# Loading half of y from ScalarE's queue, x's first rows last, and releasing the stores by a product

## The chip, the core and the metric

The kernel runs on one core of a Trainium2 chip. The metric is the device time of one execution in microseconds (us); three runs of the kernel before gave 119.63, 119.76 and 119.88, a median of 119.76. A core has compute engines with an instruction stream each: TensorE (PE in the profile), VectorE (DVE), ScalarE (ACT), GpSimd (POOL) and SyncE (SP). Data moves between the chip's main memory (HBM) and the on-chip memory (SBUF, 128 partitions) through 16 DMA engines. SP and ACT each own a DMA queue; an instruction on SP or ACT puts one transfer into its queue, where all 16 DMA engines work on it. Engines wait for each other and for transfers through semaphores.

## The reference

`x` and `y` are bf16 arrays of 1024 x 16 x 512, `gamma` is a bf16 row of 512. The result is

```python
def reference(x, y, gamma):
    return x + gamma * y
```

So 16.78 MB of `x` and 16.78 MB of `y` are read and 16.78 MB are written. Per element there is one product and one sum.

## The kernel before

The 16384 rows of 512 elements are spread over the 128 partitions, 128 rows for each partition (1 KB a row). "Row" below means such a row of a partition, 0 to 127, so a row stands for 128 KB over all partitions. `BLOCKS` (line 7) cuts HBM in three, so that a partition's rows 0 to 4, 4 to 68 and 68 to 128 each lie together in HBM. A transfer takes part or all of one block, and in one partition it is a single run of bytes: 4 KB for rows 0 to 4, 64 KB for rows 4 to 68.

All of `y` has its place in SBUF (`y_sb`, 128 rows) and is overwritten first by the product and then by the sum; stores go out of it. `x` has only 76 rows of space (`x_sb`); the last number of an `x` load in the lists is the row of `x_sb` at which it lands, so later loads of `x` reuse the place of earlier ones and have to wait for the sums that read those.

Four lists are the whole schedule.

- `SP` (line 12) is the order in which SP issues transfers: y 0-4, y 4-68, x 4-68, y 68-128, x 68-120, x 120-128. `ring` (line 113) writes them out. For an `x` load it waits for the sums that free its place (line 126): x 68-120 for the sum of rows 24 to 68, and x 120-128 for the sum of rows 0 to 8.
- `ACT` (line 20) is ACT's order: x 0-4, gamma, and then the stores of rows 4-68, 0-4 and 68-128.
- `PIECES` (line 9) cuts the rows for VectorE into 0-8, 8-24, 24-68, 68-120 and 120-128, and `DVE` (line 28) is the order of its products ('m', line 180) and sums ('a', line 189): products 0, 1, 2; sums 2, 0, 1; products 3, 4; sums 3, 4.
- `EARLY` (line 22) says how many issues of SP and of ACT are put at the very start of the program, ahead of the engines' common start. `HOLD` and `AHEAD` (line 24) hold SP's third and ACT's second issue, and the first product, until y 0-4 has landed: TensorE waits for that landing (line 147) and then tells SP, ACT and VectorE (line 149).

`gamma` lands as a single row on one partition. TensorE multiplies it by a column of ones (line 152), so that it stands in all 128 partitions of PSUM, and VectorE copies it to `gamma_sb` (line 154). No product can start before that copy.

The stores are kept back by `RELEASE` (line 26). TensorE waits until x 68-120 has landed (line 157) and then raises `s_go`, for which ACT waits ahead of its first store (line 123), and `s_rel`, for which VectorE waits ahead of the sum of rows 68-120 (line 167). Beside that each store waits for the sums of its rows.

Of the kernel before, what the change touches and what calls it, by code (L numbers as in the profile page):

```python
# [5 lines left out]

BLOCKS = [4, 64, 60]

PIECES = [8, 16, 44, 52, 8]


SP = [
    ('y', 0, 4),
    ('y', 4, 68),
    ('x', 4, 68, 4),
    ('y', 68, 128),
    ('x', 68, 120, 24),
    ('x', 120, 128, 0),
]
ACT = [('x', 0, 4, 0), ('g',), ('s', 4, 68), ('s', 0, 4), ('s', 68, 128)]  # L20

EARLY = (2, 1)

HOLD, AHEAD = ('y', 0, 4), (2, 1)

RELEASE = ('x', 68, 120, 24)

DVE = [('m', 0), ('m', 1), ('m', 2), ('a', 2), ('a', 0), ('a', 1), ('m', 3), ('m', 4), ('a', 3), ('a', 4)]
MULT, ADD = mybir.AluOpType.mult, mybir.AluOpType.add


def _take(sem, n, eng):


    return eng.wait_ge(sem, n).then_inc(sem, -n)  # L35


def kernel(
    tc: tile.TileContext,
    x: bass.AP,  # L40
    y: bass.AP,
    gamma: bass.AP,
    out: bass.AP,
):

    nc = tc.nc
    P = nc.NUM_PARTITIONS
    tc.close()  # L50
    tc.compile()  # L51

    xf = x.flatten_outer_dims()
    yf = y.flatten_outer_dims()
    of = out.flatten_outer_dims()
    N, D = xf.shape
    rows = N // P
    n = len(PIECES)
    assert sum(PIECES) == rows
    starts = [sum(PIECES[:c]) for c in range(n + 1)]  # L60
    dt = xf.dtype
    edges = [sum(BLOCKS[:c]) for c in range(len(BLOCKS) + 1)]
    assert edges[-1] == rows

    def rows_of(t, a, b):

        c = max(c for c in range(len(BLOCKS)) if edges[c] <= a)
        assert b <= edges[c + 1]
        block = t[P * edges[c] : P * edges[c + 1]].rearrange("(p n) d -> p n d", p=P)
        return block[:, a - edges[c] : b - edges[c], :]  # L70

    gamma_row = nc.alloc_sbuf_tensor("gamma_row", [1, D], dt).ap()
    ones_row = nc.alloc_sbuf_tensor("ones_row", [1, P], dt).ap()
    gamma_sb = nc.alloc_sbuf_tensor("gamma_sb", [P, D], dt).ap()
    y_sb = nc.alloc_sbuf_tensor("y_sb", [P, rows, D], dt).ap()
    x_loads = [w for w in ACT + SP if w[0] == "x"]
    y_loads = [w for w in SP + ACT if w[0] == "y"]
    stores = [w for w in SP + ACT if w[0] == "s"]
    for loads in (x_loads, y_loads, stores):
        assert sum(w[2] - w[1] for w in loads) == rows  # L80
    x_rows = max(w[3] + w[2] - w[1] for w in x_loads)
    x_sb = nc.alloc_sbuf_tensor("x_sb", [P, x_rows, D], dt).ap()
    gamma_ps = nc.alloc_psum_tensor("gamma_ps", [P, D], mybir.dt.float32).ap()

    sem = nc.alloc_semaphore
    s_gamma, s_ones, s_ps, s_dve = sem("s_gamma"), sem("s_ones"), sem("s_ps"), sem("s_dve")
    s_load = {w: sem("s_" + "_".join(map(str, w[:2]))) for w in x_loads + y_loads}
    s_held = {nc.sync: sem("s_held_sp"), nc.scalar: sem("s_held_act"), nc.vector: sem("s_held_dve")}
    s_add, s_go, s_rel, s_end, s_out = sem("s_add"), sem("s_go"), sem("s_rel"), sem("s_end"), sem("s_out")
    added = [a for kind, *a in DVE if kind == "a"]  # L90
    order = {a[0]: k for k, a in enumerate(added)}

    def meets(a, b, c, d):
        return a < d and c < b

    def pieces_of(a, b):
        return [c for c in range(n) if meets(starts[c], starts[c + 1], a, b)]

    def x_at(row):
        return next(w[3] + row - w[1] for w in x_loads if w[1] <= row < w[2])  # L100

    def frees(w):

        c = set()
        for v in x_loads[: x_loads.index(w)]:
            lo, hi = max(v[3], w[3]), min(v[3] + v[2] - v[1], w[3] + w[2] - w[1])
            if lo < hi:
                c |= set(pieces_of(v[1] + lo - v[3], v[1] + hi - v[3]))
        return sorted(c)

    early = []

    def ring(eng, what, n_early, n_ahead):

        known, went = 0, False
        for k, w in enumerate(what):
            kind = w[0]
            if k == n_ahead:
                _take(s_held[eng], 1, eng)
            need = frees(w) if kind == "x" else pieces_of(w[1], w[2]) + list(w[3:]) if kind == "s" else []  # L120
            need = max((order[c] + 1 for c in need), default=0)
            if kind == "s" and not went:
                _take(s_go, 1, eng)
                went = True
            if need > known:
                eng.wait_ge(s_add, need)
                known = need
            if kind == "g":
                i = eng.dma_start(out=gamma_row, in_=gamma.unsqueeze(0)).then_inc(s_gamma, 16)
            elif kind == "x":  # L130
                to = x_sb[:, w[3] : w[3] + w[2] - w[1], :]
                i = eng.dma_start(out=to, in_=rows_of(xf, w[1], w[2])).then_inc(s_load[w], 16)
            elif kind == "y":
                r = slice(w[1], w[2])
                i = eng.dma_start(out=y_sb[:, r, :], in_=rows_of(yf, w[1], w[2])).then_inc(s_load[w], 16)
            else:
                r = slice(w[1], w[2])
                i = eng.dma_start(out=rows_of(of, w[1], w[2]), in_=y_sb[:, r, :]).then_inc(s_out, 16)
            if k < n_early:
                early.append(i.ins)  # L140

    ring(nc.sync, SP, EARLY[0], AHEAD[0])
    ring(nc.scalar, ACT, EARLY[1], AHEAD[1])


    nc.vector.memset(ones_row, 1.0).then_inc(s_ones, 1)  # L146
    _take(s_load[HOLD], 16, nc.tensor)
    for s_one in s_held.values():
        nc.tensor.sem_inc(s_one, 1)
    _take(s_ones, 1, nc.tensor)  # L150
    _take(s_gamma, 16, nc.tensor)
    nc.tensor.matmul(gamma_ps, ones_row, gamma_row, start=True, stop=True).then_inc(s_ps, 1)  # L152
    _take(s_ps, 1, nc.vector)
    nc.vector.tensor_copy(out=gamma_sb, in_=gamma_ps).then_inc(s_dve, 1)  # L154
    _take(s_dve, 1, nc.vector)

    _take(s_load[RELEASE], 16, nc.tensor)
    nc.tensor.sem_inc(s_go, 1)
    nc.tensor.sem_inc(s_rel, 1)

    landed, open_mults = set(), 0

    def need(loads, c):
        for w in loads:
            if w not in landed and meets(starts[c], starts[c + 1], w[1], w[2]):
                if w == RELEASE:
                    _take(s_rel, 1, nc.vector)
                elif w == HOLD:
                    _take(s_held[nc.vector], 1, nc.vector)
                else:  # L170
                    _take(s_load[w], 16, nc.vector)
                landed.add(w)

    for kind, *args in DVE:
        c = args[0]
        yt = y_sb[:, starts[c] : starts[c + 1], :]
        if kind == "m":
            need(y_loads, c)
            g = gamma_sb[:, None, :].to_broadcast([P, PIECES[c], D])
            nc.vector.tensor_tensor(out=yt, in0=yt, in1=g, op=MULT).then_inc(s_dve, 1)  # L180
            open_mults += 1
        else:
            need(x_loads, c)
            if open_mults:
                _take(s_dve, open_mults, nc.vector)
                open_mults = 0
            at = x_at(starts[c])
            xt = x_sb[:, at : at + PIECES[c], :]
            nc.vector.tensor_tensor(out=yt, in0=xt, in1=yt, op=ADD).then_inc(s_add, 1)  # L189


    nc.scalar.sem_inc(s_end, 1)
    _take(s_end, 1, nc.sync)
    _take(s_add, n, nc.sync)
    _take(s_out, 16 * len(stores), nc.sync)

    main = nc.main_func.blocks[0].instructions
    names = {i.name for i in early}
    for b in nc.main_func.blocks[1:]:
        for i in [i for i in b.instructions if i.name in names]:  # L200
            b.instructions.remove(i)
    for k, i in enumerate(early):
        main.insert(1 + k, i)
# [30 lines left out]
```

## Time and profile before

| What | Value |
|---|---|
| Time, three runs | 119.63, 119.76, 119.88 us, median 119.76 |
| Span of the profiled execution, first to last instruction | 118.2 us |
| What lies around the span, against the median | 1.5 us |
| DVE busy | 70.1 us, 59% of the span, 12 instructions |
| PE busy | 0.6 us |
| DMA | 50.33 MB, 426 GB/s over the span |
| DMA time in SP's queue (q1) and ACT's (q10) | 64.8% and 33.9% of the span |
| Under way longest: y 68-128, from issue to landing | 57.3 us |

The profile gives the span of the one execution that was profiled; its own device time is not listed apart, so the 1.5 us come from the median of the three timed runs. In the profile, "L180" is line 180 of the kernel, "q1" is SP's DMA queue and "q10" is ACT's. A DMA issue on SP or ACT is only the short instruction that starts a transfer; the transfer itself stands in the DMA rows, and the list of issues gives the time from an issue to the landing of its data.

### The profile page before, as it was taken

The page shows a single profiled execution, that of the slowest core. Times are in us where ns is not written, and L with a number is a line of the kernel's source. Part 1 is how long each engine was busy: PE and PEld are TensorE (multiplying, and loading weights), DVE is VectorE, ACT ScalarE, POOL GpSimd, SP SyncE. Part 2 cuts the span into 40 slices and gives each one's busy share as a digit, 9 for nine tenths or more (in the row PEclk, how much of TensorE's full clock was granted, in tenths as well). Part 3 has the DMA queues.
Part 4 walks back from the last instruction along what each step waited for, and adds up shares of the span by engine and source line. Part 5 has one row for each costly group of instructions (what it writes and reads, how often), then busy time and mean ns, then how long its engine had stood idle before and what let it go on. Part 6 is the DMA issues. An engine that isn't in the chain of part 4 may idle for free. (4 is left out here: it accounts for less than half of the span.)

```text
span 118.2 us, 91 instructions
## 1 busy us (share of the span) xinstructions
PE 0.6 (0%) x1; PEld 0.1 (0%) x1; DVE 70.1 (59%) x12; POOL 0.2 (0%) x4
## 2 busy tenths in 40 slices
PE   0000100000000000000000000000000000000000
PEld 0000000000000000000000000000000000000000
DVE  0000200089999969999999999999999900000000
POOL 0000000000000000000000000000000000000000
DMA  6999889988899879879969696898899889799793
GB/s 248 461 666 399 355 355 399 665 355 355 355 599 466 355 333 624 374 333 499 499 288 576 288 576 288 360 637 355 355 576 488 355 355 510 333 582 416 333 499 166
DMA packets 1442, 50.33 MB, mean 426 GB/s; under 512 B 161, under 2 KB 162, under 8 KB 546
## 3 DMA queue, kind: packets, MB, share of 16 engines
q1 hardware_dynamic: 864, 33.03, 64.8%
q10 hardware_dynamic: 578, 17.30, 33.9%
HBM read 33.56 MB, written 16.78 MB: 426 GB/s over the span
## 5 line engine op out<-in xcount | busy, mean ns | idle before, releaser
L180 DVE TENSOR_TENSOR y_sb<-y_sb,gamma_sb 128x4096 bf16<-128x4096 bf16 (+3 forms) x5 | 34.7, 6981 | 10.9 <-DVEq L35 10.9
L189 DVE TENSOR_TENSOR y_sb<-x_sb,y_sb 128x4096 bf16<-128x4096 bf16 (+3 forms) x5 | 34.7, 6981 | 1.2 <-DVEq L35 1.1
L154 DVE CAST gamma_sb<-gamma_ps 128x512 bf16<-128x512 f32 x1 | 0.7, 692 | 10.2 <-DVEq L35 10.2
L146 DVE MEMSET ones_row<- 1x128 bf16 x1 | 0.2, 165 | 2.0 <-PEq L51 2.0
L152 PE MATMUL gamma_ps<-gamma_row,ones_row 1*128 1x512 bf16 x1 | 0.6, 581 | 11.6 <-PEq L35 11.6
L152 PEld LDWEIGHTS gamma_ps<-gamma_row,ones_row 1*128 1x128 bf16 x1 | 0.1, 101 | 11.6 <-issue 11.6
L218 POOL MEMSET const-bfloat16-1.0<- 128x1 bf16 x1 | 0.1, 101 | 0.0
L218 POOL MEMSET const-uint8-127<- 128x1 uint8 x1 | 0.1, 101 | 0.0
L218 POOL MEMSET const-float32-0.0<- 128x1 f32 x1 | 0.1, 98 | 0.2 <-issue 0.2
L218 POOL MEMSET const-float32-1.0<- 128x1 f32 x1 | 0.1, 98 | 0.0
## 6 DMA issues: line engine op xcount, KB each, us to landing
y_sb<-in_y_dram SPq DMA_DIRECT2D x1, 7680.0 KB, 57.3
out_dram<-y_sb ACTq DMA_DIRECT2D x1, 7680.0 KB, 23.8
x_sb<-in_x_dram SPq DMA_DIRECT2D x1, 6656.0 KB, 21.7
x_sb<-in_x_dram SPq DMA_DIRECT2D x1, 1024.0 KB, 22.0
y_sb<-in_y_dram SPq DMA_DIRECT2D x1, 512.0 KB, 3.4
x_sb<-in_x_dram ACTq DMA_DIRECT2D x1, 512.0 KB, 4.2
out_dram<-y_sb ACTq DMA_DIRECT2D x1, 512.0 KB, 22.3
y_sb<-in_y_dram SPq DMA_DIRECT2D x1, 23.4
```

The lines of the kernel that those rows point to most:

```text
L146: nc.vector.memset(ones_row, 1.0).then_inc(s_ones, 1)
L152: nc.tensor.matmul(gamma_ps, ones_row, gamma_row, start=True, stop=True).then_inc(s_ps, 1)
L154: nc.vector.tensor_copy(out=gamma_sb, in_=gamma_ps).then_inc(s_dve, 1)
L180: nc.vector.tensor_tensor(out=yt, in0=yt, in1=g, op=MULT).then_inc(s_dve, 1)
L189: nc.vector.tensor_tensor(out=yt, in0=xt, in1=yt, op=ADD).then_inc(s_add, 1)
L218: nc = _bacc.Bacc("TRN2", target_bir_lowering=False, num_devices=1)
```

## The change

Rows of `x` and `y` are loaded in another order and from other queues, and VectorE's pieces are cut to suit.

- ACT's first instruction, put at the start of the program, now loads y 4-68 (8 MB). It was SP's second. ACT's list goes on with gamma and the stores of 4-68, 68-128 and 0-4.
- SP issues y 0-4 at the start, and then, held until y 0-4 has landed, x 4-68, y 68-128, x 68-128 in one transfer, and x 0-4 last. ACT's gamma is held by the same landing, as before. x 68-128 has to wait for the sum of rows 20-68, and x 0-4 for that of rows 4-20.
- VectorE's pieces are 0-4, 4-20, 20-68 and 68-128. Its order is products 0, 1, 2; sums 2, 1; product 3; sum 3; sum 0.
- The stores are released by the end of the product of rows 68-128 (piece 3): that product raises `s_go`, and ACT and VectorE wait for `s_go` without TensorE in between. TensorE's wait for a load of `x`, and `s_rel`, go.

```diff
-PIECES = [8, 16, 44, 52, 8]
+PIECES = [4, 16, 48, 60]
 SP = [
     ('y', 0, 4),
-    ('y', 4, 68),
-    ('x', 4, 68, 4),
+    ('x', 4, 68, 0),
     ('y', 68, 128),
-    ('x', 68, 120, 24),
-    ('x', 120, 128, 0),
+    ('x', 68, 128, 16),
+    ('x', 0, 4, 0),
 ]
-ACT = [('x', 0, 4, 0), ('g',), ('s', 4, 68), ('s', 0, 4), ('s', 68, 128)]
-EARLY = (2, 1)
-HOLD, AHEAD = ('y', 0, 4), (2, 1)
-RELEASE = ('x', 68, 120, 24)
-DVE = [('m', 0), ('m', 1), ('m', 2), ('a', 2), ('a', 0), ('a', 1), ('m', 3), ('m', 4), ('a', 3), ('a', 4)]
+ACT = [('y', 4, 68), ('g',), ('s', 4, 68), ('s', 68, 128), ('s', 0, 4)]
+EARLY = (1, 1)
+HOLD, AHEAD = ('y', 0, 4), (1, 1)
+RELEASE = 3
+DVE = [('m', 0), ('m', 1), ('m', 2), ('a', 2), ('a', 1), ('m', 3), ('a', 3), ('a', 0)]
...
             if kind == "s" and not went:
-                _take(s_go, 1, eng)
+                eng.wait_ge(s_go, 1)
...
-    _take(s_load[RELEASE], 16, nc.tensor)
-    nc.tensor.sem_inc(s_go, 1)
-    nc.tensor.sem_inc(s_rel, 1)
...
-                if w == RELEASE:
-                    _take(s_rel, 1, nc.vector)
-                elif w == HOLD:
+                if w == HOLD:
...
-            nc.vector.tensor_tensor(out=yt, in0=yt, in1=g, op=MULT).then_inc(s_dve, 1)
-            open_mults += 1
+            nc.vector.tensor_tensor(out=yt, in0=yt, in1=g, op=MULT).then_inc(s_go if c == RELEASE else s_dve, 1)
+            if c == RELEASE:
+                going = True
+            else:
+                open_mults += 1
...
+            if going:
+                nc.vector.wait_ge(s_go, 1)
+                going = False
...
     _take(s_add, n, nc.sync)
+    _take(s_go, 1, nc.sync)
```

## The prediction

> **What bounds the kernel now.** I read the page first, then the issues in order of time, then the packets of short stretches. The page's span, its DMA line over 40 slices and its queue rows:
>
> ```profile
> span 118.2 us, 91 instructions
> DMA  6999889988899879879969696898899889799793
> q1 hardware_dynamic: 864, 33.03, 64.8%
> q10 hardware_dynamic: 578, 17.30, 33.9%
> ```
>
> The two queues fill 98.7% of the 16 engines' span, 50.33 MB at 426 GB/s. VectorE is busy 70.1 us, 59%. So the time is a start of 1.0 us, the bytes without a gap, and the last landing. There is almost nothing to win; what can be lost is an idle stretch of the DMA engines. The timeline shows what keeps them fed:
>
> ```profile
> 0.00 0.85 SPq L135 DMA_DIRECT2D y_sb<-in_y_dram  x2
> 0.13 0.38 ACTq L132 DMA_DIRECT2D x_sb<-in_x_dram  x1
> 3.71 0.33 SPq L132 DMA_DIRECT2D x_sb<-in_x_dram  x1
> 3.90 0.50 ACTq L129 DMA_DIRECT2D gamma_row<-in_gamma_dram  x1
> ...
> 11.59 0.58 PE L152 MATMUL gamma_ps<-gamma_row,ones_row 1*128 1x512 bf16 x1 [11.59 <-PEq L35]
> 12.32 0.69 DVE L154 CAST gamma_sb<-gamma_ps 128x512 bf16<-128x512 f32 x1 [10.16 <-DVEq L35]
> 23.95 18.43 DVE L180 TENSOR_TENSOR y_sb<-y_sb,gamma_sb 128x4096 bf16<-128x4096 bf16 x3 [10.94 <-DVEq L35]
> 43.45 18.43 DVE L189 TENSOR_TENSOR y_sb<-x_sb,y_sb 128x22528 bf16<-128x22528 bf16 x3 [1.08 <-DVEq L35]
> 55.37 2.53 SPq L132 DMA_DIRECT2D x_sb<-in_x_dram  x2
> 61.80 16.22 DVE L180 TENSOR_TENSOR y_sb<-y_sb,gamma_sb 128x26624 bf16<-128x26624 bf16 x2
> 77.41 17.36 ACTq L138 DMA_DIRECT2D out_dram<-y_sb  x3
> ```
>
> VectorE has gamma at 13.0 and waits for y 4-68 until 23.8. The load that reuses x's place is issued at 55.4, when the sum that frees it ends. From the list of issues, with times to landing:
>
> ```profile
> y_sb<-in_y_dram SPq DMA_DIRECT2D x1, 7680.0 KB, 57.3
> ...
> y_sb<-in_y_dram SPq DMA_DIRECT2D x1, 23.4
> x_sb<-in_x_dram SPq DMA_DIRECT2D x1, 39.5
> ```
>
> y 68-128 was issued at 4.1 and lands at 61.4, so that load came 6 us ahead of an empty queue. That is the slack the change can use up. y 4-68 lands at 0.4 + 23.4 = 23.8 and x 4-68 at 3.7 + 39.5 = 43.2: 19.4 us for eight 64 KB packets on each engine, **2.42 us a packet**. y 68-128 gives 18.2 / 8 = 2.27 for 60 KB.
>
> Whether two queues share the engines decides this change, and three stretches show it. Packets by queue, first between 2.2 and 3.0 us, then 8.5 to 8.8, then 11.0 to 11.3:
>
> ```profile
> q10 hardware_dynamic: 56, 0.23, 72.4%
> q1 hardware_dynamic: 41, 0.11, 33.3%
> ```
> ```profile
> q1 hardware_dynamic: 12, 0.79, 607.2%
> q10 hardware_dynamic: 1, 0.00, 1.0%
> ```
> ```profile
> q1 hardware_dynamic: 12, 0.79, 606.0%
> q10 hardware_dynamic: 1, 0.00, 0.2%
> ```
>
> Before 2.2 only q1 has packets (102). Then x 0-4 appears in q10 while 26 of y 0-4's 128 data packets remain, and both run side by side. Gamma's 1 KB packet is the single q10 packet near 8.6, its semaphore write the one near 11.1: one 64 KB packet of y 4-68 lies between the two, and 16 more packets of q1 on every engine had been issued before or with it. So **the queues take turns, packet by packet**, whatever the sizes; and gamma, issued by 4.4, was passed over by the packet that started near 6.1: one packet is drawn ahead.
>
> **The change, step by step.** *y 0-4.* y 4-68 takes x 0-4's place as ACT's first issue, so I let it start at 2.2. On average 26 / 16 = 1.6 of y 0-4's packets are left on each engine then; landing needs all 16, so I take 2 on the slowest. Two packets and the semaphore write each wait a turn of 2.42: 2.2 + 3 x 2.42 + 0.3 = 9.8, landed about 10.1 (now 3.4). Bounds: 3.4 if y 4-68 comes later than x 0-4 did; 22 if it comes at once (8 turns and more).
>
> *The hold.* SP issues x 4-68 0.3 us after that landing, at 10.4; a first packet follows an issue's start by 1.0 (0.00 to 1.0 at the beginning), so 11.4. y's fifth packet, from 12.2, is drawn already. x starts at 14.6, three of y's eight packets left. y 68-128 and, on ACT, gamma are issued just behind; nothing is idle.
>
> *gamma.* It is queued behind y 4-68 in q10 and shares the engines with x 4-68 in q1. Three pairs of turns: y's data end at 14.6 + 6 x 2.42 = 29.1. Then three turns of x, ahead of y's semaphore write, gamma and gamma's own write: 36.4. Now that write is at 11.1, so gamma is 25 us later. Bounds by the turns: with y 0-4 landed at 3.4, x starts near 7.1, y ends at 36.2 and gamma's write at 43.4; with y 0-4 landed very late, or y's write and gamma without turns of their own, near 29.
>
> *VectorE.* Matmul and copy follow gamma's write as now: 11.1 to 13.0, and 0.3 to a product: 36.4 + 2.2 = 38.6. The same 68 rows in three products take the same 18.4: 57.0. The sum of 48 rows: 52 rows take 14.02 and 44 take 11.89 (groups by shape), 0.267 a row, so 12.96, with 0.1 for its wait: 70.1. Now the freeing sum ends at 55.4.
>
> *The gap.* x 68-128 is issued at 70.1, its first packet at 71.1. y 68-128 ends at 61.4 less the 1.2 of x 0-4 that is no longer ahead, 60.2. SP's x 0-4 stands behind the waiting issue, ACT's stores behind `s_go`: **the DMA engines idle 10.9 us**.
>
> *Release.* The loads end at 71.1 + 8 x 2.27 + 1.3 (8 packets of 0.16 for x 0-4) = 90.6. VectorE: 70.1 + 4.3 (sum of 16 rows) + 16.1 (product of 60, 11.89 + 16 x 0.267) = 90.5. The release by a product instead of a landing through TensorE (77.1 to 77.4 now) saves 0.2 of hand-over, but the store's first packet comes 1.0 after its issue at 90.65, so at 91.65, 1 us behind the loads. That start is hidden now, since the last load is still moving.
>
> *Stores.* First packet to last landing is 39.5 now (78.7 to 118.2). After: 131.15. The sum of 68-128 starts at 90.7 (its x has landed near 90, its wait for `s_go` follows a product that just ended), ends at 106.8, and that of 0-4 at 108.0, ahead of 111 when the first store's data end: hidden under that store by 3 us. The small store of 0-4 moves from second to last place; its 1.3 us count in either. One load less on SP saves an issue of 0.33 inside a wait: nothing.
>
> Span 131.2, plus the 1.5 that the median before (119.76) has over its span: **132.7 us**.
>
> The Trainium skill ("DMA: Bandwidth & Descriptors", section Queues, rings and completion order) says that an engine drains a whole packet of typically 9 to 17 descriptors from one row before it switches. Gamma's data and write, split by a 64 KB piece of the other queue, speak against it here. By that rule x 4-68's eight pieces would go in one turn ahead of gamma, at about 42, and the total, an estimate from that rule, would be near 138.
>
> **Rivals.**
> 1. *Another number of turns.* Each moves gamma, and all behind it, by 2.4: 130.3 or 135.1 for one; 139.7 if y 0-4 lands at 3.4 as now (gamma at 43.4), 126 if y's write and gamma need no turns of their own or y 0-4 lands very late. For it: the 1.6 packets are a mean. Against the ends: x 0-4 did meet y 0-4's last packets.
> 2. *Gamma arrives with y 4-68* (the other side). If ACT's ring is drained first and x 4-68 follows it, gamma's write is near 23 and the first product near 25. The freeing sum then ends at 25 + 18.4 + 13 = 56.6, ahead of the queue's end at 60.2; no gap. The product of 68-128 ends at about 77.5, 2 us before the loads do, and the stores follow without a break. Time 119.5, within 0.3 either way: fewer 8 KB packets and a shorter hand-over against 4 KB packets at both ends. It decides if gamma's write comes before about 25.9 (56.6 may slip to 59.2). Against it: gamma now waits for the other queue's packets twice.
> 3. *The release's own price.* It is 1.0 as worked out, if VectorE's product ends with the loads, and nothing if the product ends a microsecond sooner against them (131.7): the two sums above differ by 0.1 only, so either can be. It lies inside the first case.
>
> **How the numbers follow.** Three turns as worked out, 132.7: 0.40. Other turn numbers, 126 to 139.7: 0.47. Gamma in time, 119.5: 0.13, of which faster by over 0.2% 0.06, within it 0.05, slower 0.02 (0.2%, 0.24 us, is about what a measurement of this kernel can tell from no change). So slower 0.89, same 0.05, faster 0.06. The range of the first two cases, 126 to 139.8, leaves out 0.13.
>
> **What would show it.** Right: y 0-4's landing near 10; x 4-68 and y 4-68 in both queues in the same slices between 15 and 29; the matmul near 37; the first product near 38.6; about three zero slices in the DMA line between 60 and 71; x 68-128's issue at the end of a sum near 70. Wrong: a matmul before 26, or y 4-68 landing before x 4-68 has a packet.

## The result and the profile after

The kernel after takes 132.59 us (four runs, 132.38 to 132.77), the kernel before 119.72. The ratio is 1.107, with a 95% interval of 1.106 to 1.109; forecast were 132.7 us. The profiled execution took 132.53 us, with a span of 131.2; so 1.3 us lie around the span, not the 1.5 that I carried over. Where a comparison below gives a range and no ratio, its executions lay too far apart for one. The page of after, its span, its DMA line and its queue rows:

```profile
span 131.2 us, 84 instructions
DMA  9789799799796996960009679699979879697793
q1 hardware_dynamic: 720, 25.17, 45.2%
q10 hardware_dynamic: 578, 25.17, 44.5%
```

The bytes are the same as before; the queues now fill 89.7% of the span instead of 98.7%. A slice is 3.3 us, and the three zeros are the slices from 59 to 69 us, in which the engines have nothing to move. The timeline of after, start and duration first:

```profile
10.98 0.33 SPq L131 DMA_DIRECT2D x_sb<-in_x_dram  x1
11.18 0.50 ACTq L128 DMA_DIRECT2D gamma_row<-in_gamma_dram  x1
...
37.06 0.58 PE L151 MATMUL gamma_ps<-gamma_row,ones_row 1*128 1x512 bf16 x1 [37.06 <-PEq L34]
...
38.74 18.43 DVE L173 TENSOR_TENSOR y_sb<-y_sb,gamma_sb 128x2048 bf16<-128x2048 bf16 x3 [0.26 <-DVEq L34]
57.31 17.29 DVE L188 TENSOR_TENSOR y_sb<-x_sb,y_sb 128x24576 bf16<-128x24576 bf16 x2
70.30 4.66 SPq L131 DMA_DIRECT2D x_sb<-in_x_dram  x2
74.52 16.15 DVE L173 TENSOR_TENSOR y_sb<-y_sb,gamma_sb 128x30720 bf16<-128x30720 bf16 x1
90.71 18.46 ACTq L137 DMA_DIRECT2D out_dram<-y_sb  x3
91.33 17.29 DVE L188 TENSOR_TENSOR y_sb<-x_sb,y_sb 128x30720 bf16<-128x30720 bf16 x2 [0.66 <-DVEq L34]
```

x 4-68 is issued at 10.98 instead of 3.71, the matmul that spreads gamma runs at 37.06 instead of 11.59, the products start at 38.74 instead of 23.95, and x 68-128 can be issued at 70.30, when the sum of rows 20-68 ends. From the list of issues of after, time to landing last (y 68-128, y 0-4, y 4-68, x 4-68):

```profile
y_sb<-in_y_dram SPq DMA_DIRECT2D x1, 7680.0 KB, 48.9
...
y_sb<-in_y_dram SPq DMA_DIRECT2D x1, 512.0 KB, 10.7
...
y_sb<-in_y_dram ACTq DMA_DIRECT2D x1, 32.3
x_sb<-in_x_dram SPq DMA_DIRECT2D x1, 31.1
```

y 4-68 lands at 32.4 (23.8 before) and x 4-68 at 42.1. y 68-128, issued at 11.4, lands at 60.2, and the next load is issued 10 us later. The turns can be counted. Packets of after by queue, between 4.5 and 7.0, 7.0 and 9.6, and 9.6 and 12.2 us, and then over 14 to 24:

```profile
q10 hardware_dynamic: 16, 1.05, 97.9%
q1 hardware_dynamic: 16, 0.07, 6.7%
```
```profile
q10 hardware_dynamic: 16, 1.05, 93.3%
q1 hardware_dynamic: 16, 0.07, 6.1%
```
```profile
q10 hardware_dynamic: 16, 1.05, 93.7%
q1 hardware_dynamic: 16, 0.00, 0.3%
```
```profile
q10 hardware_dynamic: 32, 2.10, 48.4%
q1 hardware_dynamic: 32, 2.10, 48.4%
```

In each of the first three stretches every one of the 16 engines moves one 64 KB packet of y 4-68 and one small one of y 0-4: its seventh data packet, its eighth, and its semaphore write, the packet with which an engine reports that its share has landed (16 writes, no bytes to speak of). So y 0-4 waited three turns, a turn being one packet of the other queue. From 14.67 on, x 4-68 and y 4-68 alternate, two packets each in ten us.

### The profile page after: what moved, and what is told of

Read it like the earlier page. It is cut to its first block, busy times and chain, and to the rows that moved or that the text cites. A ratio compares the mean times of both kernels' runs of the same rounds, so it can differ in the third digit from the quotient of the medians.

```text
span 131.2 us, 84 instructions
## 1 busy us (share of the span) xinstructions
PE 0.6 (0%) x1; PEld 0.1 (0%) x1; DVE 69.9 (53%) x10; POOL 0.2 (0%) x4
## 5 line engine op out<-in xcount | busy, mean ns | idle before, releaser
L188 DVE TENSOR_TENSOR y_sb<-x_sb,y_sb 128x24576 bf16<-128x24576 bf16 (+3 forms) x4 | 34.6, 8688 | 0.8 <-DVEq L34 0.7
L173 DVE TENSOR_TENSOR y_sb<-y_sb,gamma_sb 128x2048 bf16<-128x2048 bf16 (+3 forms) x4 | 34.6, 8686 | 0.3 <-DVEq L34 0.3
## 6 DMA issues: line engine op xcount, KB each, us to landing
y_sb<-in_y_dram SPq DMA_DIRECT2D x1, 512.0 KB, 10.7
```

## The experiments

Twelve kernels were run. Diffs are against the kernel named in the expectation.

**y 4-68 back on SP's queue**, all else of the change kept.

```diff
     ('y', 0, 4),
+    ('y', 4, 68),
     ('x', 4, 68, 0),
-ACT = [('y', 4, 68), ('g',), ...
-EARLY = (1, 1)
-HOLD, AHEAD = ('y', 0, 4), (1, 1)
+ACT = [('g',), ...
+EARLY = (2, 0)
+HOLD, AHEAD = ('y', 0, 4), (2, 0)
```

> The kernel after with y 4-68 back on SP's queue behind y 0-4 and gamma alone at the head of ACT's; pieces, single load of x 68-128, x 0-4 last and the release by the product stay. Theory (gamma and y 4-68 are late because two queues take turns): gamma lands near 11, first long product at 22.6, the freeing sum ends near 55, no idle DMA slice, 119.5 us. Rival A (the loss is in the new pieces, the single load, the last place of x 0-4 or the release): it stays within a few us of 132.6.

Measured: 120.34 us, ratio to before 1.0044 (1.0031 to 1.0056). Its page and timeline:

```profile
DMA  9888998889988997997797797798999889979974
```
```profile
10.53 0.58 PE L152 MATMUL gamma_ps<-gamma_row,ones_row 1*128 1x512 bf16 x1 [10.53 <-PEq L35]
...
23.11 17.29 DVE L174 TENSOR_TENSOR y_sb<-y_sb,gamma_sb 128x8192 bf16<-128x8192 bf16 x2 [9.68 <-DVEq L35]
...
55.56 4.66 SPq L132 DMA_DIRECT2D x_sb<-in_x_dram  x2
```

No zero slice is left, and 12.3 of the 12.9 us are gone. The loss is in the queue of y 4-68; rival A falls. The last 0.5 us are taken up below.

**Only gamma moved**, to SP ahead of x 4-68.

```diff
     ('y', 0, 4),
+    ('g',),
     ('x', 4, 68, 0),
-ACT = [('y', 4, 68), ('g',), ...
+ACT = [('y', 4, 68), ...
```

> The kernel after with only gamma moved, to SP's queue ahead of x 4-68; y 4-68 stays on ACT's. Theory: gamma lands near 17.5, y 4-68 still at 32.4 because it still takes turns with x 4-68; then y's landing, not gamma's, starts the long products at 32.5; the freeing sum ends at 62.9 (7.4 sooner) and the time is 125.1 us: gamma's place is 7.4 of the 12.9 us, the shared turns of y itself most of the rest. Rival B (gamma's place in the queue is all of it): 119.5 us. Rival A: 132.6.

Measured: 125.79, 127.96, 128.02 and 128.66 us; the first is the profiled one. From its timeline:

```profile
17.87 0.58 PE L152 MATMUL gamma_ps<-gamma_row,ones_row 1*128 1x512 bf16 x1 [17.87 <-PEq L35]
...
32.75 17.30 DVE L174 TENSOR_TENSOR y_sb<-y_sb,gamma_sb 128x8192 bf16<-128x8192 bf16 x2 [11.97 <-DVEq L35]
```

Gamma is there 19 us sooner, but VectorE then waits 12 us for y 4-68, whose landing is as late as in after. Rival B falls: gamma's place is about half of the loss at most. The other three executions are 2.2 us or more above the first, about one turn; only the first has a profile, so that this is a turn is argued, not shown.

**Gamma first of all.** Gamma ahead of y 4-68 on ACT.

```diff
-ACT = [('y', 4, 68), ('g',), ...
-EARLY = (1, 1)
-HOLD, AHEAD = ('y', 0, 4), (1, 1)
+ACT = [('g',), ('y', 4, 68), ...
+EARLY = (1, 2)
+HOLD, AHEAD = ('y', 0, 4), (1, 2)
```

> The kernel after with gamma ahead of y 4-68 in ACT's list, both at the start of the program; so y 4-68 is issued 0.5 us later. Theory: gamma lands near 4, but y 4-68 now reaches the engines when y 0-4's packets are through; y 0-4 lands near 3.3, SP issues x 4-68 at 3.6, x starts at 7.7 with two of y's eight packets done, and the other six each wait a turn: y 4-68 lands at 39.5 and starts the long products at 39.6 (39.9 in after). The early gamma is worth almost nothing: 132.3, or 134.7 with one turn more. Rival B (gamma's place in the queue is the whole cost): 119.5 us.

Measured: 133.08 us (132.66 to 134.03; ratio to before 1.112, 1.108 to 1.116). From the timeline of the profiled execution, which took 134.03:

```profile
4.14 0.58 PE L151 MATMUL gamma_ps<-gamma_row,ones_row 1*128 1x512 bf16 x1 [4.14 <-PEq L34]
...
41.28 17.29 DVE L173 TENSOR_TENSOR y_sb<-y_sb,gamma_sb 128x8192 bf16<-128x8192 bf16 x2 [34.23 <-DVEq L34]
```

With gamma 33 us sooner than in after, the time is about the same. Since y 4-68 is issued half a microsecond later, y 0-4 escapes its turns and lands at 3.2, so x 4-68 starts at 7.5 and takes turns with six of y's packets instead of three. The late landing of y 4-68 does alone what gamma does in after.

**No second queue beside the end of y 4-68.** y 4-68 and gamma on ACT as in after, but x 4-68 held until y 4-68 has landed.

```diff
-HOLD, AHEAD = ('y', 0, 4), (1, 1)
+HOLD, AHEAD = ('y', 4, 68), (1, 2)
```

> The kernel after with y 4-68 first and gamma behind it in ACT's queue as it is, but x 4-68 held until y 4-68 has landed, so that no second queue takes turns with it. Theory: y 4-68 lands at 22.5, gamma with it, first product near 25, freeing sum ends at 57; the DMA engines idle some 2 us from 22 to 24 because x 4-68 is issued only then; 121.5 to 122.2 us. If gamma's place behind 8 MB were the cost by itself, with or without turns (rival B), the time would stay near 132.6.

Measured: 122.76 us (ratio to before 1.0243, 1.0229 to 1.0257). Its timeline:

```profile
23.26 0.33 SPq L131 DMA_DIRECT2D x_sb<-in_x_dram  x1
...
23.86 0.58 PE L151 MATMUL gamma_ps<-gamma_row,ones_row 1*128 1x512 bf16 x1 [23.86 <-PEq L34]
...
58.38 4.66 SPq L131 DMA_DIRECT2D x_sb<-in_x_dram  x2
```

Gamma is still queued behind 8 MB on ACT, yet its matmul runs at 23.9: its packet starts at 22.12, directly behind y's last. y 0-4 still lands only at 10.9, but from then on there is no second queue, and neither y's writes nor gamma wait for a turn. Most of the remaining 3 us is the stop between 22.6 and 24.2, in which no load is queued, and the slow first packets after it (2.5 to 3.5 us instead of 2.42).

**Packet sizes.** y 4-68 in two loads, so that its packets have 32 KB.

```diff
-ACT = [('y', 4, 68), ('g',), ...
-EARLY = (1, 1)
-HOLD, AHEAD = ('y', 0, 4), (1, 1)
+ACT = [('y', 4, 36), ('y', 36, 68), ('g',), ...
+EARLY = (1, 2)
+HOLD, AHEAD = ('y', 0, 4), (1, 2)
```

> The kernel after with y 4-68 in two loads on ACT, so that its packets are 32 KB where x 4-68's are 64 KB. Theory (turns by packet, whatever the size): y 0-4 lands sooner, near 7, x starts near 9.5, and y, which now gets one third of the bytes, ends near 48, gamma's write near 55, first product near 57: about 151 us, far slower. Rival C (the queues share the engines by bytes): y ends near 34, gamma soon after, about 131 us.

Measured: 144.44 to 149.15 us, the first profiled. Packets by queue between 14 and 24 us, to be held against the same stretch of after above:

```profile
q1 hardware_dynamic: 48, 3.15, 72.6%
q10 hardware_dynamic: 51, 1.15, 26.6%
```

About as many packets in both queues (16 of q10's 51 are the semaphore writes of the first half, which take turns too), and so 3.15 MB of x beside 1.15 MB of y, where after has 2.10 and 2.10. Turns go by packets, not by bytes; rival C falls. Gamma's write was at 48.4 instead of near 55: x came only at 11.2, not near 9.5, and y had seven or eight of its 16 packets through by then.

**The mirror image**, x 4-68 in two loads beside y's 64 KB packets.

```diff
-    ('x', 4, 68, 0),
+    ('x', 4, 36, 0),
+    ('x', 36, 68, 32),
```

> The kernel after with x 4-68 in two loads on SP, so that x's packets are 32 KB (1.21 us a turn) beside y 4-68's 64 KB. Theory (turns by packet): from x's start at 14.6, y's last three packets end at 25.5, gamma's write follows three short turns later at 29.2 instead of 36.6, everything after it is 7.2 us sooner: 125.3 us. Rival C (shared by bytes): unchanged, 132.6.

Measured: 126.56 us (ratio to before 1.056, 1.051 to 1.060). Shorter packets of the other queue shorten the turns: 6.0 us less than after. I had 7.2; in this kernel y 0-4 waited for two turns, not three, and x started earlier (12.3), so that it met four of y's packets instead of three. That takes back 1.4 on gamma's write (30.6 for 29.2).

**The release undone**, with after's lists and TensorE's wait for x 68-128 as in before.

```diff
-RELEASE = 3
+RELEASE = ('x', 68, 128, 16)
...
+    _take(s_load[RELEASE], 16, nc.tensor)
+    nc.tensor.sem_inc(s_go, 1)
+    nc.tensor.sem_inc(s_rel, 1)
```

> The kernel after with only the release undone: x 68-128's landing, through TensorE, releases the stores, not the end of y's last product. In the trace of after that landing is at 91.2, the product's end at 90.67, and loads move until 92.1. Theory: the release is worth under 1 us here; stores issue at 91.55, first packet 92.6, 0.5 to 1.0 us slower than after: 133.1 to 133.6. Rival D (the release by the product costs much of the 12.9 us, because it comes late): clearly faster than 132.6.

Measured: 135.68 us (135.62 to 135.95; ratio to before 1.134, 1.133 to 1.136), 3.1 slower than after where I expected under 1. Its timeline, and its packets between 7.0 and 9.6 us:

```profile
8.80 0.33 SPq L131 DMA_DIRECT2D x_sb<-in_x_dram  x1
...
39.54 0.58 PE L151 MATMUL gamma_ps<-gamma_row,ones_row 1*128 1x512 bf16 x1 [39.54 <-PEq L34]
...
94.08 18.15 ACTq L137 DMA_DIRECT2D out_dram<-y_sb  x3
```
```profile
q10 hardware_dynamic: 16, 1.05, 93.5%
q1 hardware_dynamic: 16, 0.00, 0.3%
```

Here the 16 semaphore writes of y 0-4 stand where after still has its eighth data packet: y 4-68 first appears at 2.33, not 2.19, seven packets of y 0-4 were through instead of six, and it waited two turns. x starts a turn sooner, meets four of y's packets instead of three, and the matmul is 2.48 us **later**. That leaves 0.6 for the release. So the comparison mixed two things, and the same edit was made to the kernel with y 4-68 on SP, where no two big loads meet:

> The kernel with y 4-68 back on SP and gamma at the head of ACT's queue (120.34 us), with the release undone as well: x 68-128's landing, through TensorE, releases the stores. Here nothing takes turns at the start, so the turn count cannot blur the comparison. In the trace of the kernel with y on SP, that landing is at 78.6, the product's end at 76.8, x 0-4's last packets move until 80. Theory: stores issue at 79.0 instead of 76.8, the first comes at 80, so the engines that are done with x 0-4 at 79.0 idle up to 1 us: 0.5 to 1.0 us slower than 120.34, that is 120.8 to 121.3. If the release by the product costs instead of helping: at or below 120.3.

Measured: 120.43 us, ratio to before 1.0062 (1.0045 to 1.0078), against 1.0044 (1.0031 to 1.0056) with the release by the product. The intervals overlap: the release is worth 0.1 to 0.2 us or nothing, not my 0.5 to 1.0. The stores come 0.8 us later for the first engines, but then all 16 start together.

**Late gamma alone, in the kernel before.** Gamma on SP's queue, first directly behind y 4-68, then behind x 4-68.

```diff
     ('y', 4, 68),
+    ('g',),
     ('x', 4, 68, 4),
-ACT = [('x', 0, 4, 0), ('g',), ...
+ACT = [('x', 0, 4, 0), ...
```

```diff
     ('x', 4, 68, 4),
+    ('g',),
     ('y', 68, 128),
-ACT = [('x', 0, 4, 0), ('g',), ...
+ACT = [('x', 0, 4, 0), ...
```

> The kernel before with only gamma moved: to SP's queue directly behind y 4-68 and ahead of x 4-68; no second queue is busy. Theory: gamma lands at 23.5, just behind y 4-68, the first product starts near 25.6 instead of 23.9, the freeing sum ends near 56 and the queue runs until 61: no gap, 119.7 us, the same. Rival B (gamma behind 8 MB costs by itself): slower by 2 us or more.

> The kernel before with gamma moved one place further, behind x 4-68 on SP's queue; all else as before. Theory (a late gamma is enough for the whole loss, with the old pieces, the old release and one queue): gamma lands near 43, first product near 45, freeing sum ends at 75.4, the DMA engines idle from 61 to 76.5, loads end near 95: about 135.5 us. Rival A (the loss needs the other parts of the change): under 125.

Measured: 119.77 us (ratio 1.0002, 0.9993 to 1.0011) and 136.78 (1.143, 1.142 to 1.145). The first kernel's timeline, then the second's, and the second's DMA line:

```profile
23.88 0.58 PE L153 MATMUL gamma_ps<-gamma_row,ones_row 1*128 1x512 bf16 x1 [23.88 <-PEq L36]
...
56.16 2.53 SPq L133 DMA_DIRECT2D x_sb<-in_x_dram  x2
```
```profile
43.33 0.58 PE L153 MATMUL gamma_ps<-gamma_row,ones_row 1*128 1x512 bf16 x1 [43.33 <-PEq L36]
...
75.61 2.53 SPq L133 DMA_DIRECT2D x_sb<-in_x_dram  x2
```
```profile
DMA  6979979799796989860000779996997977999976
```

Gamma 12 us later moves the products by 1.7 us (they wait for y anyway) and the freeing sum by 0.8, and costs nothing as long as that sum ends before the queue is empty. Gamma 32 us later opens a gap of four slices, with the old pieces and the old release.

**The last 0.5 us** of the kernel with y on SP. Two kernels put x 0-4 back at the start.

The first has other pieces, so that x 68-128 needs the sum of rows 16-68 alone:

```diff
-PIECES = [4, 16, 48, 60]
+PIECES = [4, 12, 52, 60]
-    ('x', 4, 68, 0),
+    ('y', 4, 68),
+    ('x', 4, 68, 4),
...
-    ('x', 0, 4, 0),
-ACT = [('y', 4, 68), ('g',), ('s', 4, 68), ('s', 68, 128), ('s', 0, 4)]
+ACT = [('x', 0, 4, 0), ('g',), ('s', 4, 68), ('s', 0, 4), ('s', 68, 128)]
-DVE = [..., ('a', 2), ('a', 1), ('m', 3), ('a', 3), ('a', 0)]
+DVE = [..., ('a', 2), ('a', 0), ('a', 1), ('m', 3), ('a', 3)]
```

The second keeps after's pieces and puts x 0-4 elsewhere:

```diff
+    ('y', 4, 68),
     ('x', 4, 68, 0),
...
-    ('x', 0, 4, 0),
-ACT = [('y', 4, 68), ('g',), ('s', 4, 68), ('s', 68, 128), ('s', 0, 4)]
+ACT = [('x', 0, 4, 72), ('g',), ('s', 4, 68), ('s', 0, 4), ('s', 68, 128)]
-DVE = [('m', 0), ('m', 1), ('m', 2), ('a', 2), ('a', 1), ('m', 3), ('a', 3), ('a', 0)]
+DVE = [('m', 0), ('a', 0), ('m', 1), ('m', 2), ('a', 2), ('a', 1), ('m', 3), ('a', 3)]
```

Both have EARLY and AHEAD of before.

> The kernel after with y 4-68 back on SP and x 0-4 back as ACT's first load; x 68-128 in one load and the release by y's last product stay (pieces 4, 12, 52, 60, so that x 68-128 needs one sum only). It asks which part of the change still costs 0.5 us where y is on SP (120.34). Theory now: x 0-4's small packets, last and beside the first stores, spread the 16 engines apart (0.96 us between the first and the last end, 0.43 in before). Then this kernel is at 119.6 to 119.8, level with before. Rival: the single load or the release costs it; then it stays at 120.3.

> As the run with x 0-4 early, but with the pieces of after (4, 16, 48, 60), x 0-4 in x's last 4 rows and its sum right after its product, so that x 68-128 is again issued some 4.5 us before the queue ahead of it is empty (that run: 57.7 against a last packet that starts at 58.5, and 121.15 us). Theory L (a load issued with less than about one packet in hand spreads the engines, and that was that run's loss; x 0-4 in the last place costs the 0.5 us of the kernel with y on SP): 119.6 to 119.9. Theory R (the release by the product or the single load costs the 0.5): 120.3. If the lead does not matter: near 121.2.

Measured: 121.15 us (ratio 1.0112, 1.0087 to 1.0137) and 120.69 (1.0073, 1.0059 to 1.0087). Neither came down to 119.7, and the second's number is none of the three that I had written. The second kernel's first store, then its store packets between 78.9 and 81.8, then those of before between 78.7 and 81.6, the same 2.9 us from the first:

```profile
77.84 18.48 ACTq L137 DMA_DIRECT2D out_dram<-y_sb  x3
```
```profile
q10 hardware_dynamic: 16, 1.05, 113.0%
```
```profile
q10 hardware_dynamic: 32, 2.10, 166.8%
```

In before every engine has begun its second 64 KB of stores by then, here none: the first packets took 3.0 to 3.6 us instead of 2.42 (2.5 to 3.5 in the first kernel). In the second kernel this is nearly the whole loss: on the last engine its loads end 0.1 us later than in before (79.29 and 79.16), its stores 1.0 later (118.85 and 117.85). So these two kernels lose time in a new place and do not decide whether x 0-4's last place costs the 0.5.

Why those first packets are slow stays open. The stores were issued 1.1 us before the first engine's loads ran out (77.84 and 78.92), in before 1.3 (77.41 and 78.73); but a short lead is not the cause by itself. In after it was 0.5 (90.71 and 91.23), and in the kernel with y on SP and the release undone the stores were issued when the first loads had already run out (78.88 and 78.82). The first packets of both took 2.42 to 2.47 us. The last kernel's store packets in the 2.9 us from its first, 79.7 to 82.6:

```profile
q10 hardware_dynamic: 32, 2.10, 168.4%
```

The traces do say where the kernel with y on SP is slower. On the last engine its stores begin at 79.96, in before at 79.16. About half of these 0.8 us is lost before 23 us: y 4-68 lands at 23.0, 0.8 sooner than in before, though the 1.3 us of x 0-4 no longer went ahead. The rest comes while x 0-4 moves with the stores already issued: the 16 engines end x 68-128 within 0.5 us of each other (77.66 to 78.20) and x 0-4 within 1.0 (78.97 to 79.96). With the release undone they end x 0-4 within 0.5 (78.82 to 79.36), but the stores then come too late to gain from it. Why the start is slower stays open.

## Why the prediction was right

- *Turns on y 0-4*: three, as chosen; landing 10.7 for 10.1. The first small packets took up to 0.5 us each, and on the last engine y 4-68 began at 2.67 instead of 2.2. That it was three was luck in part: 0.14 us later, in the kernel with the release undone, it was two.
- *The hold and x's start*: issue 10.98 for 10.4, first packet of x 14.67 for 14.6, with five of y's packets through, the fifth drawn ahead. Right.
- *gamma*: y's data end at 29.2 (29.1), y's write comes at 31.6, gamma at 34.1 and its write at 36.59 (36.4). That writes and small packets each wait a full turn was the step with most at stake, and it held.
- *VectorE*: first product 38.74 (38.6), freeing sum's end 70.28 (70.1).
- *The gap*, 10.9 forecast: from 59.4-59.9 to 71.3-72.0, about 11.9 on an engine. Too small by 1: I let it begin at the landing of y 68-128 (60.2, as forecast), but the last data had moved 0.6 earlier on average, and the load's first packets came 0.4 later than forecast. They also took 2.8 to 3.4 us on 15 of the 16 engines instead of 2.27, so the loads end at 92.1 on the last engine instead of 90.6.
- *The release*, 1.0 forecast: about nothing. The product ended at 90.67 as worked out (90.5), the first store packet came at 91.58 (91.65), but loads were still moving until 92.1. The end of the product fixes when the stores can start, so the longer gap and the slow packets only filled the time that I had put down to the release. The sum is right, its split is not; had the loads run another microsecond late, the span (131.2 for 131.2) would have been missed, so it is right partly by luck.
- *The time around the span*, 1.5: 1.3 in the profiled execution.
- *Rivals.* The first, another number of turns, is real: the kernel with the release undone is one turn off, at 135.7 (I had 135.1 for one). In the second I named gamma's write before 25.9 as the point that decides. As a test by itself that is wrong: with gamma's matmul at 4.1 or 17.9 the time is still 126 to 134, because y 4-68 lands late by its own turns, in after only some 5 us ahead of gamma. Both have to come early.
- *Side sums.* The lower end of the range does not follow from its own bound: gamma's write near 29, 7.3 sooner than 36.4, gives 125.4, not 126. In the second rival the product of 68-128 would end at 77.0 (56.6 + 4.3 + 16.1), not 77.5. Neither bears on the forecast.

The Trainium skill ("DMA: Bandwidth & Descriptors", section Issuing engines are not separate DMA queues) says that transfers started by different engines run on the same 16 DMA engines and interleave. The equal packet counts of after between 14 and 24 us agree. The other rule weighed in the prediction, 9 to 17 descriptors in a turn, does not fit here, if a packet of the profile is one descriptor: the kernel with 32 KB packets alternates one by one, and in after gamma's write came at 36.6, not near 42.

## What to carry to other kernels

Here two queues shared the engines packet by packet, so a load that something waits for should not stand beside big packets of another queue, or behind packets that take turns with them. Splitting the loads over two queues brought no bandwidth (a 64 KB packet took 2.42 us either way) and delayed the one that was needed first. What a delay costs is read from the slack of the load it feeds: 12 us on gamma cost nothing while the queue was still full, and 32 us cost 17. Where one transfer arrives just as another ends, the outcome jumps by whole turns: undoing the release, far behind in the program, moved the time by 3.1 us, 2.5 of them by a turn.

## What the runs showed of the hardware

- A semaphore write waits for a turn of its own: those of y 0-4 came 2.4 us behind its last data packet, with one packet of y 4-68 between.
- A tenth of a microsecond in the arrival of y 4-68 went with a whole turn: where its first packet started at 2.19 (after), 2.24 (gamma moved to SP) or 2.30 (x 4-68 held), y 0-4 waited three turns, and at 2.33 (release undone) or 2.46 (x 4-68 in halves) two. With the release undone the shorter wait made the kernel slower, since x 4-68 then met four of y's packets instead of three.
- Loads restarted slowly after a stop: the first packets took 2.8 to 3.4 us for 60 KB on 15 of 16 engines in after (a stop of 12 us) and 2.5 to 3.5 for 64 KB where x 4-68 was held (a stop of about 2 us), against 2.27 and 2.42. Stores that began 0.4 us or more after the loads had run out, in the kernel with y on SP and the release undone, did not: 2.45 to 2.46.
